# A chunked linear-attention and MLP kernel: the third pair's loads reordered and gated behind a second-stage product, three buffers of stacked v, and a new hand-written order

## The chip, the cores and the metric

The kernel runs on one core of one Trainium2 chip. The metric is device time in microseconds (us). TensorE (PE in the profile) multiplies matrices, VectorE (DVE), ScalarE (ACT) and GpSimd (POOL) do the elementwise work, and SyncE (SP) issues most of the DMA transfers. All engines run beside each other, each one in its own program order, and wait for one another through semaphores.

## The reference

Two stages follow each other. First a recurrent attention with decay, over 4 batches, 8 heads, 768 tokens and a head size of 48; then a two-layer MLP with the gate h * cos(h) on all 3072 tokens.

```
for t in range(S):
    state = alpha[:, :, t, :, None] * state + einsum('bhd,bhe->bhde', k[:, :, t], v[:, :, t])
    y[:, :, t] = einsum('bhd,bhde->bhe', q[:, :, t], state)
x = y.transpose(0, 2, 1, 3).reshape(3072, 384)
h = x @ w_in            # 384 x 2048
out = (h * cos(h)) @ w_out   # 2048 x 384
```

## The kernel before

The 3072 tokens are cut into 12 pairs J of two chunks, 256 tokens each, three pairs to a batch. On the partitions lie 128 pairs of neighbouring tokens e = 0, 1; the chunk c is a half of the partitions, 64 rows each. The steps of one pair, by the names that the plan uses, are these.

- `load` (L110) brings alpha (`a`), k, q and v, 384 KB each, in one DMA each from SP's queue. `w1` (L126) and `w2` (L132) bring the weights in four quarters each, issued by GpSimd, which also changes them to bf16.
- `ln` (L146) takes the logarithm of alpha, `cums0` and `cums` (L168, L182) sum it over the tokens with triangular matrices on TensorE, and `icp`, `exps` (L209, L219) exponentiate the sums. For pairs from 3 on, `eb` bundles these and the next pair's `ln`, `mula` (L154) multiplies neighbouring alphas ahead of it, and `sub` (L199) takes one alpha off again.
- `sk` (L233) and `sq` (L237) scale k and q into the tiles kh and qh, on DVE or POOL, once for each e. `castv` (L240) casts v.
- `trans` (L288) transposes kh and qh with 32 small matmuls into PSUM, and `evT` (L294) copies each chunk out. `scores` (L303) multiplies them, `mask` (L309) applies the causal mask on DVE.
- `outer` (L321) makes the sums of k times v, `add` (L335, L337) adds the state before, and `state` (L343) decays it on POOL.
- v is stacked in another order for the last product: by four SP DMAs (`vst`, L246) or, for the first three pairs, by TensorE and a copy (`vpe` L256, `vev` L260). Two buffers `vs` hold it; a buffer is free again when the `yT` that reads it is done.
- `yT` (L370) makes the attention's output, transposed, and `evy` (L379) copies it to bf16.
- `m1` (L390) is a first-stage product: for each pair four units u, of 12 matmuls 128x128 by 128x256 each. `sin` (L396) takes the cosine on ACT, `gate` (L401) multiplies on DVE. `m2` (L419) is the second stage: for each pair two tiles c, each in four parts of four matmuls. `evo` (L431) copies the result out and `out` (L437) stores it.
- `idle` (L445) are products on zeros that keep TensorE busy at the start.

In PSUM, three buffers of two banks with the tag `h` serve the transposes, the scores, the sums, yT and the first-stage products in turn: a step that wants one waits until the reader of the buffer has finished, and a first-stage product's buffer becomes free with its gate.

The order is written out by hand. The table `PLAN` gives each step of each pair a number; all steps are sorted by it and issued in that order, with `:A` or `:D` naming another engine than the usual one. The numbers are no times: they only set the program order on every engine and on SP's and POOL's DMA queues. `GATES` makes one load wait for a step on TensorE, and since SP works in order, all loads behind it wait as well. The tile pools decide on further waits: the raw k, q and v have three buffers each and alpha four.

On ACT, logarithm and exponential belong to one table and the cosine to another; going over from one to the other costs a table load (L141 and L396).

Of the kernel before, what the change touches and what calls it, by code (L numbers as in the profile page):

```python
# [16 lines left out]
def kernel(  # L17
# [26 lines left out]
    NL, NQ, NV, NS = 4, 3, 3, 2  # L44
# [35 lines left out]
    for lst, nm, n in ((lna_t, "lna", NL), (kh_t, "kh", NQ), (qh_t, "qh", NQ), (vp_t, "vp", NV)):  # L80
        for r in range(n):
            t = consts.tile([C, 2, H, 64], BF, tag=f"{nm}{r}", name=f"{nm}{r}")
            nc.vector.memset(t[:, :, :, D:64], 0.0)
            lst.append(t)
# [14 lines left out]
    GATES, AFTER = {("a", 2): ("yT", 1)}, {}  # L99
# [7 lines left out]
    def load(nm, J):  # L107
        b, g = J // NJB, J % NJB
        t = sb.tile([C, H, 2, D], FP, tag=nm, name=nm, bufs=BUF["a" if nm == "a" else "in"])
        dma = nc.sync.dma_start(  # L110
# [120 lines left out]
    def scale_k(J, e, eng):  # L231
        icp_ = icp_sb.pop((J, e)).rearrange("p (h d) -> p h d", h=H)
        eng.tensor_tensor(out=kh_t[J % NQ][:, e, :, 0:D], in0=kqv["k", J][:, :, e], in1=icp_, op=ALU.mult)  # L233

    def scale_q(J, e, eng):
        cp = cp_sb[J, e][:, 0:HD].rearrange("p (h d) -> p h d", h=H)
        eng.tensor_tensor(out=qh_t[J % NQ][:, e, :, 0:D], in0=kqv["q", J][:, :, e], in1=cp, op=ALU.mult)  # L237
# [43 lines left out]
    def trans(J):  # L281
        T_ps[J] = ps.tile([C, 2, 2 * NP, 2, HC], BF, tag="h", name="T_ps", bufs=3)
        for i, x in ((1, kh_t[J % NQ]), (0, qh_t[J % NQ])):
            for p in range(NP):
                for e in range(2):
                    for c in range(2):
                        r = slice(HC * c, HC * c + HC)
                        last = nc.tensor.transpose(T_ps[J][:, c, i * NP + p, e, :],  # L288
                                            x[r, e, 2 * p : 2 * p + 2, :].rearrange("s h d -> s (h d)"), ident_bf[r, r])
# [23 lines left out]
    def outer(J):  # L313
# [3 lines left out]
        for p in range(NP):  # L317
            for e in range(2):
                for c in range(n):
# [3 lines left out]
                        kh[r, e, 2 * p : 2 * p + 2, :].rearrange("s h d -> s (h d)"),  # L323
# [61 lines left out]
    def mlp1(J, u):  # L385
        h_ps[J, u] = ps.tile([C, FW, T2], FP, tag="h", name="h_ps", bufs=3)
        for f in range(FW):
            ft = u * FW + f
            for kk in range(KT):
                nc.tensor.matmul(h_ps[J, u][:, f, :], w1[:, kk, ft * C : (ft + 1) * C], xT[J][:, kk, :],  # L390
                                 start=(kk == 0), stop=(kk == KT - 1))

# [15 lines left out]
    def mlp2(J, c, part):  # L408
# [8 lines left out]
        for o, cols in zip(o_ps[J, c], HALVES if last_tile else [slice(0, DM)]):  # L417
            for ft in fts:
                nc.tensor.matmul(o[:, 0 : cols.stop - cols.start], gsb[J][:, ft, c * C : (c + 1) * C], w2[:, ft, cols],  # L419
                                 start=(done == 1 and ft == fts[0]), stop=(done == MP and ft == fts[-1]))  # L420

# [19 lines left out]
    def idle(n):  # L441
# [5 lines left out]
    copies = {"DVE": nc.vector.tensor_copy, "ACT": nc.scalar.copy}  # L447
    mults = {"DVE": nc.vector, "POOL": nc.gpsimd}
    steps = {
        "load": lambda J, nm: load(nm, J), "w1": load_w1, "w2": load_w2,  # L450
# [4 lines left out]
        "evT": lambda J, c, eng="DVE": evict_T(J, c, copies[eng]), "scores": scores, "mask": mask, "outer": outer,  # L455
# [71 lines left out]
    }  # L527
    IDLE = [(45, 10), (155, 2), (345, 9), (375, 1), (435, 4), (485, 3)]
# [45 lines left out]
```

## Time and profile before

| | us |
|---|---|
| median of three runs (185.56 to 185.94) | 185.88 |
| the profiled execution | 185.78 |
| its span, first to last instruction | 184.0 |
| busy TensorE / VectorE / ScalarE / GpSimd | 173.0 / 134.5 / 124.9 / 83.5 |
| idle products on zeros, within TensorE's busy time | 9.0 |
| first first-stage product starts | 17.3 |
| last TensorE matmul ends | 180.8 |

All times in the text are counted from the span's first instruction. The profile has a page and views of the trace: busy times by stage (windows), the instructions of one engine in order of time (timeline), groups of instructions by line, tile views, and the DMA issues with the time from issue to landing. In the rows of a timeline stand start, duration, engine, line, operation, output<-inputs, their shapes, the count (x12), and in brackets how long the engine sat idle before and what ended that. In the rows of groups stand the busy time, the mean of one in ns, and the idle time before them.

### The profile page before, as it was taken

What the parts mean: (1) busy time and instruction counts of PE and PEld (TensorE: products, weight loads), DVE (VectorE), ACT (ScalarE), POOL (GpSimd) and SP (SyncE); (2) the same over time, 40 slices, a digit from 0 to 9 for tenths busy, and PEclk for the clock granted to TensorE, in tenths of its full rate; (3) what the DMA queues carried; (4) which work ended last, traced back from release to release, by engine and by line L of the source; (5) the groups of instructions that cost most, each with busy time, mean ns of one, the idle gap of its engine ahead of it and who ended that gap; (6) DMA issues with size and microseconds to landing.
All of it is one profiled execution on the core that took longest, in us unless ns stands there. A gap on an engine that the chain in (4) does not pass through costs nothing.

```text
span 184.0 us, 5742 instructions
## 1 busy us (share of the span) xinstructions
PE 173.0 (94%) x2457; PEld 125.5 (68%) x2458; DVE 134.5 (73%) x182; ACT 124.9 (68%) x157; POOL 83.5 (45%) x116
## 2 busy tenths in 40 slices
PE   7989579979999999999999999999899999999993
PEld 2445458646687776876787777876687677776672
DVE  7069777669999899799969898879587674734520
ACT  3745457789879999895978989869774517435201
POOL 5388550079883484939686093903901110000000
PEclk9999999999999999999999999999999999999999
DMA  6999999999999979963996579003420121010312
GB/s 146 261 248 224 216 202 206 262 256 257 261 213 262 304 170 278 260 164 85 278 289 154 140 215 245 18 6 88 143 71 4 41 88 51 0 43 4 127 44 86
DMA packets 60137, 29.47 MB, mean 160 GB/s; under 512 B 51024, under 2 KB 60112, under 8 KB 60112
## 3 DMA queue, kind: packets, MB, share of 16 engines
q1 hardware_dynamic: 56256, 25.86, 57.9%
q0 software_dynamic: 3712, 3.15, 10.6%
q8 instruction: 19, 0.31, 0.8%
q10 hardware_dynamic: 144, 0.10, 0.2%
q14 instruction: 6, 0.05, 0.1%
HBM read 25.17 MB, written 4.72 MB: 162 GB/s over the span
## 4 chain that ended last, share of the span: by engine, by line
PE 68%; DMA 11%; issue 7%; SPq 6%; POOL 5%; ACT 1%; DVE 1%; POOLq 0%; DVEq 0%
PE h_ps L390 28%; PE o_ps L419 26%; DMA v<-in_v_dram 6%; SPq L110 4%; PE y_ps L370 4%; DMA k<-in_k_dram 4%; PE A_ps L303 2%; PE T_ps L288 2%; PE U_ps L321 2%; SPq L246 2%; PE o_last L419 1%; DMA vs<-vp 1%; POOL un L343 1%; POOL a L154 1%; PE cums L168 1%
## 5 line engine op out<-in xcount | busy, mean ns | idle before, releaser
L401 DVE TENSOR_TENSOR gsb<-h_ps,c_sb 128x1024 bf16<-128x1024 f32 x48 | 58.4, 1222 | 20.0 <-ACT c_sb L396 18.8
L396 ACT ACTIVATE c_sb<-h_ps,halfpi 128x1024 bf16<-128x1024 f32 x48 | 53.4, 1114 | 28.5 <-PE h_ps L390 28.4
L390 PE MATMUL h_ps<-xT,w 128*128 128x256 bf16 x576 | 67.5, 273 | 0.7 <-DMA w<-in_moe_w_in_dram 0.5
L419 PE MATMUL o_ps<-w,gsb 128*128 128x384 bf16 x368 | 66.7, 326 | 0.0
L390 PEld LDWEIGHTS <-w 128*128 128x128 bf16 x576 | 55.4, 98 | 9.7 <-DMA w<-in_moe_w_in_dram 0.8
L419 PEld LDWEIGHTS <-gsb 128*128 128x128 bf16 x400 | 37.0, 98 | 20.8
L343 POOL TENSOR_TENSOR un<-us,c 128x384 bf16<-128x384 f32 x20 | 16.7, 836 | 33.1 <-DVE us L335 26.0
L309 DVE TENSOR_TENSOR A_sb<-A_ps,msk 128x1024 bf16<-128x1024 f32 x24 | 29.1, 1220 | 3.6 <-PE A_ps L303 3.4
L233 POOL TENSOR_TENSOR kh<-k,icp 128x384 bf16<-128x384 f32 x19 | 19.5, 1032 | 10.2 <-ACT lna L146 5.3
L237 POOL TENSOR_TENSOR qh<-q,cp 128x384 bf16<-128x384 f32 x19 | 18.8, 999 | 6.1 <-ACT cp L219 4.2
L154 POOL TENSOR_TENSOR a<-a 128x384 f32<-128x384 f32 x9 | 9.0, 997 | 11.8 <-DMA a<-in_alpha_dram 11.8
L240 POOL CAST vp<-v 128x768 bf16<-128x768 f32 x12 | 10.1, 853 | 6.4 <-DMA v<-in_v_dram 6.0
L146 ACT ACTIVATE lna<-a 128x768 bf16<-128x768 f32 x12 | 10.1, 842 | 4.1 <-DMA a<-in_alpha_dram 2.4
L141 ACT ACT_TABLE_LOAD x9 | 11.5, 1283 | 0.9 <-PEq L558 0.7
L294 DVE COPY qkT<-T_ps 128x1024 bf16<-128x1024 bf16 x17 | 11.4, 682 | 0.8 <-PE T_ps L288 0.8
L396 ACT ACT_TABLE_LOAD x9 | 11.5, 1283 | 0.2
L431 ACT COPY o_sb<-o_ps 128x384 f32<-128x384 f32 x10 | 4.8, 478 | 9.6 <-PE o_ps L419 9.6
L431 DVE COPY o_sb<-o_ps 128x384 f32<-128x384 f32 x13 | 7.2, 554 | 4.3 <-PE o_ps L419 4.2
L445 PE MATMUL idle_ps<-zeros 128*128 128x512 bf16 x28 | 9.0, 469 | 1.2 <-DVE halfpi L77 1.2
L379 DVE CAST xT<-y_ps 128x384 bf16<-128x384 f32 x14 | 7.7, 584 | 3.1 <-PE y_ps L370 2.9
L335 DVE TENSOR_TENSOR us<-U_ps,un 128x384 f32<-128x384 f32 x16 | 8.8, 551 | 1.3 <-PE U_ps L321 1.2
L303 PE MATMUL A_ps<-qkT 48*128 48x128 bf16 x192 | 8.7, 217 | 0.6 <-DVE qkT L294 0.5
(68 smaller groups left out, 149.2 us busy)
## 6 DMA issues: line engine op xcount, KB each, us to landing
a<-in_alpha_dram SPq DMA_DIRECT2D x12, 384.0 KB, 6.0
v<-in_v_dram SPq DMA_DIRECT2D x12, 384.0 KB, 6.1
k<-in_k_dram SPq DMA_DIRECT2D x12, 384.0 KB, 6.0
q<-in_q_dram SPq DMA_DIRECT2D x12, 384.0 KB, 6.2
out_dram<-o_sb SPq DMA_DIRECT2D x23, 192.0 KB, 2.3
vs<-vp SPq DMA_DIRECT2D x36, 64.0 KB, 2.8
w<-in_moe_w_in_dram POOLq DMA_DIRECT2D x4, 384.0 KB, 8.7
w<-in_moe_w_out_dram POOLq DMA_DIRECT2D x4, 384.0 KB, 10.7
```

What stands on the lines that cost most here:

```text
L141: nc.scalar.preload_act_table_set("natural_log_exp_and_others")
L233: eng.tensor_tensor(out=kh_t[J % NQ][:, e, :, 0:D], in0=kqv["k", J][:, :, e], in1=icp_, op=ALU.mult)
L237: eng.tensor_tensor(out=qh_t[J % NQ][:, e, :, 0:D], in0=kqv["q", J][:, :, e], in1=cp, op=ALU.mult)
L294: ins = copy(out=qkT_sb[J][:, c], in_=T_ps[J][:, c].rearrange("r n e s -> r n (e s)"))
L303: last = nc.tensor.matmul(A_ps[J, c][:, a, p, :], qkT[r, c, NP + p, :], qkT[r, c, p, :], start=True, stop=True)
L309: nc.vector.tensor_tensor(out=A_sb[J][:, c].rearrange("s a p t -> s (a p) t"), in0=A_ps.pop((J, c)).rearrange("s a p t -> s (a p) t"), in1 ...
L343: nc.gpsimd.tensor_tensor(out=u, in0=U_sum.pop(n), in1=c2_sb[J][:, :, c].unsqueeze(3).to_broadcast([C, NP, 2, D]), op=ALU.mult)
L390: nc.tensor.matmul(h_ps[J, u][:, f, :], w1[:, kk, ft * C : (ft + 1) * C], xT[J][:, kk, :], start=(kk == 0), stop=(kk == KT - 1))
L396: nc.scalar.activation(out=c_sb[J, u], in_=h_ps[J, u], func=AF.Sin, bias=halfpi, scale=1.0)
L401: nc.vector.tensor_tensor(out=gsb[J][:, u * FW : (u + 1) * FW], in0=h_ps.pop((J, u)), in1=c_sb.pop((J, u)), op=ALU.mult)
L419: nc.tensor.matmul(o[:, 0 : cols.stop - cols.start], gsb[J][:, ft, c * C : (c + 1) * C], w2[:, ft, cols], start=(done == 1 and ft == fts[0 ...
L431: copy(out=t, in_=o_ps.pop((J, c))[0][:, 0:DM])
```

## The change

- SP's first loads come in another order: v1, a1, a0, v0, k0, q0, q1, k1, a2, q2 (the number is the pair) in place of a0, a1, v0, k0, q0, k1, q1, v1, q2.
- The gate is another one. Before, a2 waited for the yT of pair 1. Now a2 and q2 wait for no step; a3, k3, q3, v3 and a4 wait for the part 3 of the second-stage product of pair 0, tile 0 (`m2 0 0 3`). On SP a3 stands before k2 and v2, which so come behind it too.
- GpSimd issues the weights in one run behind the casts of v1 and v0, with two short steps between: w1 quarters 1, 0, 3, 2, then w2 quarters 3, 2, 1, 0.
- The stacked v has three buffers in place of two (NS), with one more memset on POOL.
- kh and qh are laid out by head pair, then e, in place of e, then head.
- A step `tr` that transposes by DMA is defined, but the plan does not hold it.
- The whole plan is new: the position of every step, and the engine of some. Among others, on DVE the scaling of pair 1's k (`sk 1 1`, `sk 1 0`) comes before `mask 0 1` of pair 0; on ACT `ln 2` comes before the first cosine. 44 idle products stand in the plan in place of 29.

```
-    NL, NQ, NV, NS = 4, 3, 3, 2
+    NL, NQ, NV, NS = 4, 3, 3, 3
...
-            t = consts.tile([C, 2, H, 64], BF, tag=f"{nm}{r}", name=f"{nm}{r}")
+            t = consts.tile([C, 2, H, 64] if nm in ("lna", "vp") else [C, H, 2, 64], BF, tag=f"{nm}{r}", name=f"{nm}{r}")
             nc.vector.memset(t[:, :, :, D:64], 0.0)
-            lst.append(t)
+            lst.append(t.rearrange("s (p e) a d -> s p e a d", p=NP) if nm in ("kh", "qh") else t)
...
-    GATES, AFTER = {("a", 2): ("yT", 1)}, {}
+    GATES, AFTER = {('a', 3): ('m2', 0, 0, 3), ('k', 3): ('m2', 0, 0, 3), ('q', 3): ('m2', 0, 0, 3), ('v', 3): ('m2', 0, 0, 3), ('a', 4): ('m2', 0, 0, 3)}, {}
...
+        pass_gate(("m2", J, c, part), last)
...
-        "load a": "10 20 960 1030 1170 1450 1460 2230 2570 2290 3490 2960",
-        "load k": "70 190 1040 1270 1530 2020 1990 3050 3500 4180 3440 4290",
-        "load q": "100 230 300 1290 1620 1950 2580 2850 3980 4010 3970 4770",
-        "load v": "40 290 1130 1220 1730 1930 1940 3090 3680 2990 4970 4850",
-        "w1": "330 200 470 460 - - - - - - - -",
-        "w2": "260 580 820 690 - - - - - - - -",
+        "load a": "40 20 670 1160 1370 1780 2170 2320 2730 2910 3970 3890",
+        "load k": "200 450 1210 1470 1810 2250 2750 2760 3580 3620 4400 4680",
+        "load q": "300 410 1010 1510 1880 2220 2440 3320 3020 3720 4270 3490",
+        "load v": "90 10 1290 1710 1950 2700 2310 3650 4150 4730 5300 5110",
+        "w1": "120 110 230 220 - - - - - - - -",
+        "w2": "490 460 400 320 - - - - - - - -",
...
-        "ln": "30 110 1060 1100 - - - - - - - -",
+        "ln": "50 30 740 1180 - - - - - - - -",
...
-        "sk 1": "250 280 1350:D 1560:D 2100 2260 2890:D 3340 3890 4510 4890 5480",
+        "sk 1": "270:D 510:D 1250 1490:D 2090 2260 2900 3180:D 3960 4080 4780 4910",
...
-        "castv": "90 610 1210 1260 2120 2750 2720 3760 3730 4980 5000 5360",
+        "castv": "100 80 1300 1720 1970 3090 2860 3670 4160 4750 5310 5710",
-        "vst": "- - - 1820 2320 3120 3110 4040 4450 5160 5010 5380",
+        "vst": "- - - 2060 2280 3350 3290 4310 4770 5050 5320 5730",
...
-        "mask 1": "430 720 1600 1870 2420 3390 3540 4110 4470 5070 5100 5880",
+        "mask 1": "560 700 1450 1760 2300 3480 3430 4190 4410 5070 5470 5860",
...
-        "yT": "490 780 1750 2150 2790 3570 3620 4330 4870 5170 5670 5970",
+        "yT": "600 760 1630 2070 2650 3550 3520 4320 4950 5130 5630 5900",
...
-        "m1 0": "740 940 2000 2520 2980 3670 3900 4620 5150 5610 5900 6040",
-        "m1 1": "560 890 1960 2400 2950 3860 3750 4630 5250 5390 5850 6090",
+        "m1 0": "810 1140 1890 2430 2960 3760 3790 4590 5080 5570 5830 6390",
+        "m1 1": "710 930 1830 2670 2840 3730 3660 4740 5290 5440 6010 6080",
...
-        "sin 1": "570 900 1970 2410 2970 3870 3790 4690 5280 5400 5860 6100",
+        "sin 1": "790 940 1840 2680 2920 3740 3700 4850 5330 5450 6030 6090",
...
-        "m2 0 3": "1010 1510 2350 2770 3410 4300 4830 5440 5720 6120 6320 6550",
+        "m2 0 3": "950 1560 2370 3000 3450 4200 4940 5400 5800 6160 6340 6540",
...
-    IDLE = [(45, 10), (155, 2), (345, 9), (375, 1), (435, 4), (485, 3)]
+    IDLE = [(55, 17), (275, 7), (385, 5), (435, 6), (525, 2), (575, 5), (595, 2)]
```

More of the change, by code (lines that the diff above doesn't have):

```diff
@@ L105, in pass_gate, with load @@
                 AFTER[key] = last
-    def load(nm, J):
+    def load(nm, J, queue):
         b, g = J // NJB, J % NJB
         t = sb.tile([C, H, 2, D], FP, tag=nm, name=nm, bufs=BUF["a" if nm == "a" else "in"])
-        dma = nc.sync.dma_start(
+        dma = queue.dma_start(
             out=t.rearrange("p h e d -> p h (e d)"),
@@ L232, in scale_k @@
         icp_ = icp_sb.pop((J, e)).rearrange("p (h d) -> p h d", h=H)
-        eng.tensor_tensor(out=kh_t[J % NQ][:, e, :, 0:D], in0=kqv["k", J][:, :, e], in1=icp_, op=ALU.mult)
+        eng.tensor_tensor(out=kh_t[J % NQ][:, :, e, :, 0:D], in0=kqv["k", J][:, :, e].rearrange("p (n a) d -> p n a d", a=2),
+                          in1=icp_.rearrange("p (n a) d -> p n a d", a=2), op=ALU.mult)
     def scale_q(J, e, eng):
         cp = cp_sb[J, e][:, 0:HD].rearrange("p (h d) -> p h d", h=H)
-        eng.tensor_tensor(out=qh_t[J % NQ][:, e, :, 0:D], in0=kqv["q", J][:, :, e], in1=cp, op=ALU.mult)
+        eng.tensor_tensor(out=qh_t[J % NQ][:, :, e, :, 0:D], in0=kqv["q", J][:, :, e].rearrange("p (n a) d -> p n a d", a=2),
+                          in1=cp.rearrange("p (n a) d -> p n a d", a=2), op=ALU.mult)
     def cast_v(J):
@@ L288, in trans, with trans_dma @@
                         last = nc.tensor.transpose(T_ps[J][:, c, i * NP + p, e, :],
-                                            x[r, e, 2 * p : 2 * p + 2, :].rearrange("s h d -> s (h d)"), ident_bf[r, r])
+                                            x[r, p, e].rearrange("s a d -> s (a d)"), ident_bf[r, r])
+    def trans_dma(J, x, c):
+        if J not in qkT_sb:
+            qkT_sb[J] = sb.tile([C, 2, 2 * NP, C], BF, tag="qkT", name="qkT", bufs=BUF["qkT"])
+        r = slice(HC * c, HC * c + HC)
+        i, src_t = {"k": (1, kh_t), "q": (0, qh_t)}[x]
+        nc.sync.dma_start_transpose(
+            out=qkT_sb[J][:, c, i * NP : (i + 1) * NP, :].rearrange("r n (e s) -> r (n e) s", e=2),
+            in_=src_t[J % NQ][r].rearrange("s p e a d -> s (p e a d)"))
     def evict_T(J, c, copy):
@@ L322, in outer @@
                         U_ps[J][:, c, 2 * p * D : 2 * (p + 1) * D].rearrange("r (a d) -> r a d", a=2),
-                        kh[r, e, 2 * p : 2 * p + 2, :].rearrange("s h d -> s (h d)"),
+                        kh[r, p, e].rearrange("s a d -> s (a d)"),
                         vp[r, e, 2 * p : 2 * p + 2, 0:D], start=(e == 0), stop=(e == 1))
@@ L389, in mlp1 @@
             for kk in range(KT):
-                nc.tensor.matmul(h_ps[J, u][:, f, :], w1[:, kk, ft * C : (ft + 1) * C], xT[J][:, kk, :],
+                last = nc.tensor.matmul(h_ps[J, u][:, f, :], w1[:, kk, ft * C : (ft + 1) * C], xT[J][:, kk, :],
                                  start=(kk == 0), stop=(kk == KT - 1))
+        pass_gate(("m1", J, u), last)
     def cosine(J, u):
@@ L418, in mlp2 @@
             for ft in fts:
-                nc.tensor.matmul(o[:, 0 : cols.stop - cols.start], gsb[J][:, ft, c * C : (c + 1) * C], w2[:, ft, cols],
+                last = nc.tensor.matmul(o[:, 0 : cols.stop - cols.start], gsb[J][:, ft, c * C : (c + 1) * C], w2[:, ft, cols],
                                  start=(done == 1 and ft == fts[0]), stop=(done == MP and ft == fts[-1]))
+        pass_gate(("m2", J, c, part), last)
     def evict_o(J, c, copy):
@@ L447 @@
     copies = {"DVE": nc.vector.tensor_copy, "ACT": nc.scalar.copy}
+    queues = {"SP": nc.sync, "POOL": nc.gpsimd}
     mults = {"DVE": nc.vector, "POOL": nc.gpsimd}
     steps = {
-        "load": lambda J, nm: load(nm, J), "w1": load_w1, "w2": load_w2,
+        "load": lambda J, nm, eng="SP": load(nm, J, queues[eng]), "w1": load_w1, "w2": load_w2,
         "mula": mul_a, "ln": ln, "cums0": cums0, "cums": cums, "sub": sub, "icp": icp, "exps": exps, "eb": session,
@@ L454 @@
         "vev": lambda J, eng="DVE": evict_vs(J, copies[eng]), "decay": decay, "trans": trans,
-        "evT": lambda J, c, eng="DVE": evict_T(J, c, copies[eng]), "scores": scores, "mask": mask, "outer": outer,
+        "evT": lambda J, c, eng="DVE": evict_T(J, c, copies[eng]), "tr": trans_dma, "scores": scores, "mask": mask, "outer": outer,
         "add": add_state, "state": decay_state, "yT": yT, "evy": lambda J, c, eng="ACT": evict_y(J, c, copies[eng]),
```

96 rows, old and new, of the table PLAN are left out of this document.

## The prediction

> **What bounds the kernel now.** First the page, then the busy times by stage, then TensorE's own timeline.
>
> ```profile
> span 184.0 us, 5742 instructions
> PE 173.0 (94%) x2457; PEld 125.5 (68%) x2458; DVE 134.5 (73%) x182; ACT 124.9 (68%) x157; POOL 83.5 (45%) x116
> ```
> ```profile
> 0.00:27.15 27.15, 21.41 (x324) 12.44 (x326) 18.06 (x46) 13.83 (x20) 17.06 (x36) 1.00 1.14 216
> 27.15:34.36 7.21, 7.21 (x64) 6.28 (x65) 5.51 (x5) 5.75 (x6) 0.00 (x0) 1.00 1.24 230
> 34.36:60.00 25.64, 24.34 (x401) 17.02 (x399) 21.16 (x29) 21.73 (x30) 17.92 (x20) 1.00 1.10 249
> 120.00:130.00 10.00, 9.22 (x181) 6.11 (x179) 8.46 (x10) 8.51 (x12) 2.94 (x5) 1.00 0.25 55
> 170.00:184.00 14.00, 10.84 (x87) 7.76 (x84) 3.92 (x5) 2.15 (x4) 0.00 (x0) 0.99 0.23 84
> ```
> ```profile
> 0.00:34.36 34.36, 11.16 (x96) 7.93 (x7) 7.80 (x7) 1.00 1.16 219
> ```
> ```profile
> 24.61 0.63 PE L370 MATMUL y_ps<-A_sb,vs 128*32 128x128 bf16 x32
> 25.18 1.48 PE L390 MATMUL h_ps<-xT,w 128*128 128x256 bf16 x12
> 27.15 5.42 PE L390 MATMUL h_ps<-xT,w 128*128 128x256 bf16 x48 [0.49 <-DMA w<-in_moe_w_in_dram]
> ```
> A window's row gives its length, then PE, PEld, DVE, ACT and POOL busy, the clock, the DMA share and GB/s. TensorE (PE) sets the time. From 27.15 on it hardly stops: nothing is lost to 34.36, 1.30 us from there to 60, 0.78 in the window from 120, and 3.16 in the tail. Its work is the same matrix products in both kernels, so the change can move the end in three ways: by when PE gets going, by waits in the middle, and by that 0.78. The front is the large item: of the 21.41 busy us ahead of 27.15 much is idle products on zeros. The second fence is the window to 34.36 for the tile h_ps alone (PE, DVE, ACT): 96 matmuls, eight first-stage products of 12. Four run from 27.15 (1.31 each: 5.42 less the modelled overlap of 0.16), one more by 34.36, so three stand ahead of 27.15 and two ahead of 25.18.
>
> What sets the front is when loads land.
>
> ```profile
> 7.21 1.45 SPq L110 DMA_DIRECT2D q<-in_q_dram  x1
> 8.70 1.44 SPq L110 DMA_DIRECT2D v<-in_v_dram  x1
> 10.18 1.40 SPq L110 DMA_DIRECT2D q<-in_q_dram  x1
> ```
> ```profile
> q<-in_q_dram SPq DMA_DIRECT2D x1, 384.0 KB, 6.2
> v<-in_v_dram SPq DMA_DIRECT2D x1, 384.0 KB, 10.9
> q<-in_q_dram SPq DMA_DIRECT2D x1, 384.0 KB, 16.3
> ```
> ```profile
> 4.43 0.84 ACT L146 ACTIVATE lna<-a 128x768 bf16<-128x768 f32 x1 [2.41 <-DMA a<-in_alpha_dram]
> 7.49 0.82 POOL L240 CAST vp<-v 128x768 bf16<-128x768 f32 x1 [4.29 <-DMA v<-in_v_dram]
> 8.55 0.93 POOL L126 DMA_DIRECT2D w<-in_moe_w_in_dram  x1
> 9.03 0.56 DVE L233 TENSOR_TENSOR kh<-k,icp 128x384 bf16<-128x384 f32 x1 [4.49 <-DMA k<-in_k_dram]
> 12.09 1.95 POOL L233 TENSOR_TENSOR kh<-k,icp 128x384 bf16<-128x384 f32 x2 [0.76 <-DMA k<-in_k_dram]
> ```
> The second fence is the DMA view (KB, us from issue to landing) in the windows around the 7th, 8th and 9th issue. Loads 1, 3, 4 and 6 land at 4.43, 7.49, 9.03 and 12.09: 1.5 us apart. The 7th lands at 7.21 + 6.2 = 13.4. The 8th takes 10.9 us, to 19.6, and the 9th 16.3, to 26.5: the weights, issued by GpSimd from 8.55 on, have begun to move. The DMA queues in the windows 11 to 12, 12 to 13 and 13 to 14 (packets, MB, share) show it:
>
> ```profile
> q1 hardware_dynamic: 694, 0.26, 127.5%
> ```
> ```profile
> q1 hardware_dynamic: 407, 0.15, 74.5%
> q0 software_dynamic: 91, 0.09, 55.5%
> ```
> ```profile
> q0 software_dynamic: 201, 0.21, 123.1%
> q1 hardware_dynamic: 4, 0.00, 0.9%
> ```
> The inputs alone move 0.26 MB per us (a load is 0.39 MB); once the weights come they move nothing from 13 to 14.
>
> **The change, part by part.** *Load order.* SP now issues v1, a1, a0, v0, k0, q0, q1, k1, a2, q2, with v1 the second pair's v. The positions land as before: v0, now 4th, at 9.0, k0 at 10.5, q0 at 12.1, q1 at 13.4. k1 is 8th, in the place where v1 took until 19.6; a2 is 9th.
>
> *Weights.* They are issued behind the casts of v1 and v0 on POOL: 9.03 + 0.82 is 9.85, which is 1.3 us after 8.55. Before, their first bytes came in the window from 12 (about 12.2 by the 0.09 MB); now about 13.5. k1 then has its first 0.12 MB through at full rate. The remaining 0.27 MB, and the hole behind it, I scale from the 8th load before (6.2 us from the 7th's landing to its own): two thirds of that is 4.2, so 17.6, and I take **17.9**, between 15 (no sharing: 13.4 + 1.5) and 19.6 (as before), nearer the row that shows sharing. a2 comes 26.5 - 19.6 = 6.9 later: **24.8**, between 3 later (equal shares) and 26.5.
>
> *New order, behind k1.* On DVE, sk 1 1 waits for k1, and queued behind it are sk 1 0, add 0 0 and mask 0 1 of the *first* pair, which its yT needs. Before, that mask ran ahead of all second-pair work. Durations:
>
> ```profile
> L401 DVE TENSOR_TENSOR gsb<-h_ps,c_sb 128x1024 bf16<-128x1024 f32 x48 | 58.4, 1222 | 20.0 <-ACT c_sb L396 18.8
> L396 ACT ACTIVATE c_sb<-h_ps,halfpi 128x1024 bf16<-128x1024 f32 x48 | 53.4, 1114 | 28.5 <-PE h_ps L390 28.4
> L309 DVE TENSOR_TENSOR A_sb<-A_ps,msk 128x1024 bf16<-128x1024 f32 x24 | 29.1, 1220 | 3.6 <-PE A_ps L303 3.4
> L141 ACT ACT_TABLE_LOAD x9 | 11.5, 1283 | 0.9 <-PEq L558 0.7
> L294 ACT COPY qkT<-T_ps 128x1024 bf16<-128x1024 bf16 x7 | 7.0, 1010 | 1.9 <-PE T_ps L288 1.8
> L335 DVE TENSOR_TENSOR us<-U_ps,un 128x384 f32<-128x384 f32 x16 | 8.8, 551 | 1.3 <-PE U_ps L321 1.2
> ```
> ```profile
> 8.44 2.10 PE L445 MATMUL idle_ps<-zeros 128*128 128x512 bf16 x9
> 16.45 0.41 PE L288 MATMUL T_ps<-ident_bf,kh 64*128 64x64 bf16 x16
> 24.28 0.52 PE L370 MATMUL y_ps<-qkT,un 128*32 128x128 bf16 x24 [0.53 <-DVE A_sb L309]
> ```
> With K the landing of k1: two scalings (0.56 each, pipelined) K+1.05; the 32 transposes K+1.65; the first eviction on ACT K+2.75; scores K+3.2; two idle matmuls (0.23 each) K+3.65; yT of pair 0 to K+4.45, whose mask was ready at K+2.8 (add 0.55, mask 1.22). DVE goes add, mask 1 0 (to K+4.6), xT, add, mask 1 1 (to K+6.95); PE meanwhile does outer 1, scores and one first-stage product (to K+6.65). yT of pair 1 (0.9) ends at K+7.95 = **25.85**. Before it ended at 24.61 + 0.63 = 25.2 with two products done; now one is.
>
> *ln 2 moves ahead.* On ACT it now stands in front of the first cosine and waits for a2. Behind it: ln 0.84 (the 4.43 row), table load 1.28, cosine 1.11, then gate 1.22 on DVE: 24.8 + 4.5 = 29.3. That gate frees the PSUM buffer for the fourth product, which PE would reach at 25.85 + 2 x 1.31 = 28.45: a wait of **0.85**. Then the fourth to sixth product (3.9) and one second-stage part (0.65, half of a product, as 4 x 384 columns are to 12 x 256) end at 33.9, and the gate on SP opens. At 34.36 the old kernel had done that and two products more; it had the same work done 2.62 earlier, at 31.75. Loss: 33.9 - 31.75 = **+2.15**.
>
> *The gate.* a3 waits for that part, and all later loads stand behind it on SP, k2 and v2 among them. Before, the gate opened at the first row; the second gives the landing times of the loads of alpha:
>
> ```profile
> 25.30 0.99 SPq L110 DMA_DIRECT2D a<-in_alpha_dram  x2
> ```
> ```profile
> DMA to landing us min/median/max: 3.7/6.0/10.6
> ```
> By 33.9 the weights are nearly in (eight of 0.39 MB at 0.2 MB per us is 15.7, plus 2.7 loads of 1.5, from 13.5 on: 33.3), so a3 lands by the short end, 3.7, at 37.6, k2 at 39.1, v2 at 40.6. PE has 7.6 us of older products first (two first-stage, six second-stage, the sums), to 41.55, and sk 2 1 (1.0 on POOL) ends at 40.1: hidden, with 1.4 to spare. Three waits remain by the same reckoning: ln 3 behind two table loads and two cosines on ACT (0.5), ln 4 behind the next session (0.5), yT 2 behind four scalings on DVE (0.45). 1.45 against 1.30 before: **+0.15**.
>
> *Third stacked v.* Before, pair 10's stacking waits for yT 8, and pair 9's stands behind it on SP:
>
> ```profile
> 122.99 5.70 SPq L246 DMA_DIRECT2D vs<-vp  x8
> 130.04 0.75 PE L370 MATMUL y_ps<-A_sb,vs 128*32 128x128 bf16 x32 [0.80 <-DMA vs<-vp]
> ```
> With three buffers it needs yT 7 only: **-0.8**. The added memset (0.3) lies before the first cast, where POOL waits 4.29.
>
> *At nothing:* the layout of qh and kh (same element and instruction counts; each transpose and outer product still reads 128 adjacent columns; if the longer pattern cost POOL 0.1 us each, 33 of them would still lie in an engine 45% busy); the DMA transpose, which the plan never calls; 15 more idle matmuls (3.5 us), all beside waits but the two in the sum; five evictions of T moved to ACT (0.33 longer each), off the path after the front; the tail, whose last products and store are the same.
>
> Sum: 2.15 + 0.15 - 0.8 = **+1.5** on the profiled execution's 185.78 (span 184.0 and 1.78 around it; 0.10 under the median of 185.88): **187.3**.
>
> **Rivals.** *Equal turns, faster.* If the weights and inputs take turns evenly, the rest of k1 (0.27 MB) moves at 0.13 per us and lands by 16.5, a2 by about 20. Then DVE is the floor: mask 0 0 ends at 16.7 (q0 12.1, scaling to 13.5, transposes 14.0, eviction 15.0, scores 15.5, mask 1.22). yT 1 ends at 24.65, no wait on ACT: loss 2.15 - 1.2 - 0.85 = 0.1, in all -0.55, **185.2**. The sum turns at K = 17.25 with a2 in time. For it: from 12 to 13 both queues moved; against it: the hole from 13 to 14 and the 9th load's 16.3 us. The Trainium skill, "DMA: Bandwidth & Descriptors", section "Queues, rings and completion order", says that each DMA engine goes round the queues with work packet by packet, which would bring about this rival; the 8th and 9th load bear it out poorly. 24%.
> *The gate bites.* If weights still move when it opens, a3 takes 10.6 as before and k2 lands at 46, PE waits 4 to 5 us at trans 2: **191.5**. Against it: the DMA reckoning above. 8%.
> *Absorbed.* The middle waits are set by loads and ACT, so a PE that comes 2 us later may find them gone: -1.3, **186.0**, no difference. Against it: a3 and ln 3 come later too. 10%.
>
> **How the numbers follow.** The forecast has 58%. Its own range: K from 16.9 to 19.6, a2 to 26.5: 186.2 to 189.3. With the equal turns at the low end and some new wait of the rearranged order at the high end: **185.0 to 189.6**; the gate's 191.5 and the rest are left out. A difference under 0.2% (0.37 us) cannot be told from none here. Faster 0.18 (most of the equal turns), same 0.15 (their rest, and most of the absorbed case), slower 0.67.
>
> **What would show it.** Load 8 (k1) landing near 18 and a2 near 25; DVE idle before sk 1 1; ACT idle before ln 2 and PE before the fourth first-stage product; yT 1 ending near 26; SP's gate near 34; sk 2 without a long wait for k2; no PE wait for vs. Wrong, if k1 lands before 17, or if PE waits over 2 us between 35 and 50.

## The result and the profile after

The changed kernel takes 185.14 us (median of five runs, 184.87 to 185.21) beside 185.88 for the kernel before on the same chip (five runs, 185.56 to 185.99): a ratio of 0.9963, with a 95% interval of 0.9949 to 0.9978. That is 0.4% faster, where 187.3, slower by 0.8%, was forecast. Of the page, two lines:

```profile
span 183.4 us, 5755 instructions
PE 175.2 (96%) x2470; PEld 126.1 (69%) x2473; DVE 132.6 (72%) x182; ACT 126.0 (69%) x160; POOL 78.8 (43%) x112
```

The span is 0.6 us shorter. TensorE still sets it. The same windows as in the prediction (length, PE, PEld, DVE, ACT, POOL busy, clock, DMA share, GB/s):

```profile
0.00:27.15 27.15, 23.78 (x337) 13.30 (x341) 16.63 (x46) 13.65 (x20) 15.36 (x35) 1.00 1.13 215
27.15:34.36 7.21, 5.80 (x55) 4.74 (x55) 6.46 (x6) 5.99 (x7) 0.00 (x0) 1.00 1.14 177
34.36:60.00 25.64, 25.38 (x407) 18.21 (x406) 21.47 (x30) 23.85 (x33) 14.85 (x17) 1.00 1.10 251
120.00:130.00 10.00, 10.00 (x206) 6.73 (x204) 8.12 (x11) 8.10 (x11) 7.24 (x9) 1.00 0.37 86
```

The front does lose: TensorE stops for 1.41 us in the second window, where the old kernel lost nothing. But the third loses 0.26 instead of 1.30, and the fourth nothing instead of 0.78. The instructions behind this, from the timelines of SP, POOL, DVE, ACT and PE (start, duration, engine, line, operation, in brackets the idle time before and what ended it):

```profile
8.78 1.44 SPq L110 DMA_DIRECT2D k<-in_k_dram  x1
10.26 1.39 SPq L110 DMA_DIRECT2D a<-in_alpha_dram  x1
...
9.84 3.25 POOL L126 DMA_DIRECT2D w<-in_moe_w_in_dram  x4
...
16.63 1.02 DVE L233 TENSOR_TENSOR kh<-k,icp 128x384 bf16<-128x384 f32 x2
...
23.98 0.85 ACT L146 ACTIVATE lna<-a 128x768 bf16<-128x768 f32 x1 [2.20 <-DMA a<-in_alpha_dram]
...
23.76 0.63 PE L381 MATMUL y_ps<-A_sb,vs 128*32 128x128 bf16 x32
24.32 2.79 PE L401 MATMUL h_ps<-xT,w 128*128 128x256 bf16 x24
28.56 4.09 PE L401 MATMUL h_ps<-xT,w 128*128 128x256 bf16 x36 [1.44 <-DVE gsb L413]
32.49 0.81 PE L431 MATMUL o_ps<-w,gsb 128*128 128x384 bf16 x4
...
42.40 0.32 PE L168 MATMUL cums<-lna,tri 128*128 128x384 bf16 x1 [0.26 <-ACT lna L146]
```

The DMA view of the windows around the two issues (KB, us to landing) gives the landings:

```profile
k<-in_k_dram SPq DMA_DIRECT2D x1, 384.0 KB, 6.2
a<-in_alpha_dram SPq DMA_DIRECT2D x1, 384.0 KB, 13.7
```

k1 landed at 8.78 + 6.2 = 15.0, not at 17.9; VectorE scales it without a stop at 16.63, right behind the mask of the first pair, and yT 1 ends at 23.76 + 0.63 = 24.39, not at 25.85. a2 landed at 10.26 + 13.7 = 23.96 (24.8 forecast), ScalarE waits 2.20 for it, and through ln 2, the table load, the first cosine and its gate TensorE waits 1.44 ahead of the fourth first-stage product. The gating part of the second stage ends at 33.14 (32.49 + 0.81 less the modelled overlap of 0.16); the old kernel had that work done at 31.75: +1.39, not +2.15.

### The profile page after: what moved, and what is told of

The parts are those of the page before. It is cut to its first block, busy times and chain, and to the rows that moved or that the text cites. A ratio compares the mean times of both kernels' runs of the same rounds, so it can differ in the third digit from the quotient of the medians.

```text
span 183.4 us, 5755 instructions
## 1 busy us (share of the span) xinstructions
PE 175.2 (96%) x2470; PEld 126.1 (69%) x2473; DVE 132.6 (72%) x182; ACT 126.0 (69%) x160; POOL 78.8 (43%) x112
## 4 chain that ended last, share of the span: by engine, by line
PE 77%; DMA 7%; ACT 6%; SPq 5%; issue 1%; DVE 1%
PE h_ps L401 31%; PE o_ps L431 31%; DMA a<-in_alpha_dram 7%; SPq L110 5%; PE y_ps L381 5%; PE A_ps L314 3%; PE T_ps L290 3%; ACT c_sb L408 2%; PE U_ps L332 2%; PE o_last L431 1%; ACT L141 1%; ACT L408 1%; PE cums L168 1%; DVE gsb L413 1%; ACT lna L146 0%
## 5 line engine op out<-in xcount | busy, mean ns | idle before, releaser
L401 PEld LDWEIGHTS <-w 128*128 128x128 bf16 x576 | 55.2, 98 | 10.7 <-issue 1.9
L238 POOL TENSOR_TENSOR qh<-q,cp 128x384 bf16<-128x384 f32 x17 | 16.9, 1000 | 20.1 <-ACT cp L219 20.1
L233 POOL TENSOR_TENSOR kh<-k,icp 128x384 bf16<-128x384 f32 x16 | 16.2, 1020 | 7.5 <-DMA k<-in_k_dram 3.7
L305 ACT COPY qkT<-T_ps 128x1024 bf16<-128x1024 bf16 x12 | 11.8, 1013 | 5.7 <-PE T_ps L290 5.6
L444 ACT COPY o_sb<-o_ps 128x384 f32<-128x384 f32 x13 | 6.2, 480 | 11.1 <-PE o_ps L431 11.1
L458 PE MATMUL idle_ps<-zeros 128*128 128x512 bf16 x41 | 12.2, 442 | 1.7 <-DVE halfpi L77 1.2
L390 DVE CAST xT<-y_ps 128x384 bf16<-128x384 f32 x16 | 8.9, 586 | 3.8 <-PE y_ps L381 3.8
L233 DVE TENSOR_TENSOR kh<-k,icp 128x384 bf16<-128x384 f32 x8 | 4.2, 552 | 7.4 <-DMA k<-in_k_dram 7.4
L458 PEld LDWEIGHTS <-zeros 128*128 128x128 bf16 x44 | 4.2, 109 | 7.0 <-issue 3.0
## 6 DMA issues: line engine op xcount, KB each, us to landing
w<-in_moe_w_in_dram POOLq DMA_DIRECT2D x4, 384.0 KB, 10.7
```

Source lines behind the costliest of these rows:

```text
L233: eng.tensor_tensor(out=kh_t[J % NQ][:, :, e, :, 0:D], in0=kqv["k", J][:, :, e].rearrange("p (n a) d -> p n a d", a=2), in1=icp_.rearrange ...
L238: eng.tensor_tensor(out=qh_t[J % NQ][:, :, e, :, 0:D], in0=kqv["q", J][:, :, e].rearrange("p (n a) d -> p n a d", a=2), in1=cp.rearrange(" ...
L305: ins = copy(out=qkT_sb[J][:, c], in_=T_ps[J][:, c].rearrange("r n e s -> r n (e s)"))
L401: last = nc.tensor.matmul(h_ps[J, u][:, f, :], w1[:, kk, ft * C : (ft + 1) * C], xT[J][:, kk, :], start=(kk == 0), stop=(kk == KT - 1))
L458: nc.tensor.matmul(idle_ps[0], zeros[:, 0:C], zeros, start=True, stop=True)
```

## The experiments

The theory: the front costs 1.39, set by a2 alone; the middle gives back 1.04, because the old order's stop at cums 3 is gone; the stop for the stacked v gives about 1. The rivals: the order alone does what the third buffer is credited with; the moved gate alone empties the middle; pair 2's loads set the old middle whatever the order; the two DMA queues share by bytes. Each kernel computes everything; times are medians, the ratio is to the kernel before on the same chip. The runs stood on several chips, so that two of them are compared by their ratios or their traces. The lines of the plan are cut to the positions that differ.

**Three buffers alone, and the change without them.** The kernel before with `NS = 3`:

```
-    NL, NQ, NV, NS = 4, 3, 3, 2
+    NL, NQ, NV, NS = 4, 3, 3, 3
```

> The kernel before with three buffers of stacked v and nothing else. Theory A (the wait of 0.8 us at 130 came from the two buffers: the stacking of pair 10 waited for yT 8 and held that of pair 9 behind it on SP): the wait goes, 185.1 against 185.9. Rival B (the new order removed it, the stacking is late for another reason): the wait stays, 185.9.

184.31 us, 0.9922 (0.9905 to 0.9939): 0.8 less than expected, and more than the whole change gains. In its timeline of TensorE the stop is gone; the same product started at 130.04 in the kernel before:

```profile
128.79 0.62 PE L370 MATMUL y_ps<-A_sb,vs 128*32 128x128 bf16 x32
```

Of these 1.25 us, 0.27 were ahead already at pair 8's yT (122.06, 122.33 before); by pair 10's (144.09, 145.48 before) the buffer's share is 1.39 - 0.27 = 1.12: in the kernel before, pair 9's product starts 0.98 late (1.25 - 0.27) and takes 0.75 in place of 0.62. The opposite edit to the changed kernel, `NS = 2`:

> The changed kernel with two buffers of stacked v. Theory A (the third buffer is worth 0.8 us in the new order too): 185.9. Rival B (in the new order each stacking stands close before its own yT and after the yT two pairs earlier, so two buffers do as well): within 0.2 us of the changed kernel, 185.1.

185.05 us, 0.9971 (0.9957 to 0.9984): no different from 185.14. Its window from 120 to 130 has no stop either:

```profile
120.00:130.00 10.00, 10.00 (x217) 6.81 (x218) 8.11 (x12) 7.83 (x11) 7.24 (x9) 1.00 0.36 85
```

In the new order the third buffer is worth nothing: order and buffer remove the same stop, and either one is enough.

**The gate alone**, in the old order: a2 free, a3 behind yT 1.

```
-    GATES, AFTER = {("a", 2): ("yT", 1)}, {}
+    GATES, AFTER = {("a", 3): ("yT", 1)}, {}
```

> The kernel before with its gate moved from a2 to a3, still behind yT 1: a2 goes out early, as the tenth load. Theory A (before, PE waited 1.0 us for ln 3 because a3 stood behind a2 in a queue that the weights slowed, and landed at 36.4): a3 lands about 1.5 us earlier, ln 3 is no longer late, about 1.0 us faster, 184.9. Rival B (that wait hangs on the place of cums 3 in PE's order, a table load and mula ahead of it on ACT and POOL): the wait stays within 0.3 us, 185.6 to 185.9. A loss is possible if q2, ninth, and a2, tenth, slow the weights that PE waits for at 27.

185.85 us, 1.0022 (1.0002 to 1.0041). Its windows:

```profile
27.15:34.36 7.21, 6.37 (x57) 5.52 (x58) 4.75 (x4) 5.09 (x5) 0.00 (x0) 1.00 1.26 204
34.36:60.00 25.64, 25.24 (x408) 17.64 (x406) 21.69 (x29) 22.43 (x31) 17.70 (x20) 1.00 1.10 246
```

0.84 is lost in the front: a2 now moves beside the weights, and the last first-stage quarter, issued at about 16.4, lands 11.5 us later in place of 10.7. 0.90 is won in the middle (0.40 lost, not 1.30). Theory A's reason does not hold: a3 lands no earlier, as pair 3's `mula` on POOL shows, which waits for it (36.39 in the kernel before):

```profile
36.61 0.99 POOL L154 TENSOR_TENSOR a<-a 128x384 f32<-128x384 f32 x1 [11.32 <-DMA a<-in_alpha_dram]
```

cums 3 starts at 38.53 (38.31 before), though TensorE comes 0.84 later: a TensorE that comes later finds the old middle's stop gone.

**The weights later, in the new order.** In all three, all quarters of w1 stand behind the first pair's decay on GpSimd, which moves the first issue from 9.84 to 12.5. The first leaves three quarters of w2 right behind them:

```
-        "w1": "120 110 230 220
-        "w2": "490 460 400 320
+        "w1": "342 341 344 343
+        "w2": "490 460 400 345
```

> The changed kernel with the first five weights issued behind decay 0 on POOL, at about 12.2 in place of 9.84. Theory A (weights begin to move 4.1 us after their issue; until then inputs move at 0.26 MB per us, from then on at about 0.06): a2 is through before they begin and lands near 16.5 in place of 24.0, the cosine goes 1.7 us earlier, PE's wait of 1.4 us before the fourth first-stage product goes: 183.8. The weights land 1 to 2.4 us later and still in time. Rival B (the wait hangs on the table load behind ln 2 on ACT, or the weights come too late then): 185 or more.

184.71 us, 0.9953 (0.9938 to 0.9968), where 183.8 was expected. a2 took 6.2 us and the 1.44 were gone, but seven issues in a row hold up GpSimd's scaling of q:

```profile
19.10 0.41 PE L290 MATMUL T_ps<-ident_bf,qh 64*128 64x64 bf16 x16 [1.02 <-POOL qh L238]
```

The second has that scaling first:

```
-        "w2": "490 460 400 320
+        "w2": "490 483 482 481
```

> The changed kernel with weights behind decay 0, as in the run before, and POOL's scaling sq 1 0 ahead of the four second-stage weights. In the run before PE waited 1.0 us at the transposes of pair 1 for that scaling, which stood behind seven weights. Theory A (the front is then free of both waits): 183.7. Rival B (the second-stage weights come too late for m2 0 0 3, or ACT's chain holds the front anyway): 184.5 or more.

184.62 us, 0.9942 (0.992 to 0.9965), where 183.7 was expected. Now the first pair's state stood behind four issues and VectorE waited 1.37 for it. The third spreads them in pairs behind the states:

```
-        "w2": "490 460 400 320
+        "w2": "736 735 633 632
```

> The changed kernel with the first-stage weights behind decay 0 and sq 1 0 next, as before, and the second-stage weights in two pairs behind the states of pair 0. Before, PE gained 0.7 us of the 1.4 at the end of the front, as the first state stood behind four weights on POOL and yT 1 came 0.9 later. Theory A: yT 1 ends at 24.4 as in the changed kernel, no wait for a2, the gate opens at 31.7, 183.6. Rival B (the middle gives it back: ln 3 and the inputs of pair 2 come no earlier): the wait at cums 3 grows, 184.4 or more.

183.61 us, 0.9886 (0.9863 to 0.9909), as expected, and the best of all. Its timeline of TensorE and its windows:

```profile
24.34 6.73 PE L401 MATMUL h_ps<-xT,w 128*128 128x256 bf16 x60
30.90 0.81 PE L431 MATMUL o_ps<-w,gsb 128*128 128x384 bf16 x4
```
```profile
27.15:34.36 7.21, 7.21 (x68) 5.88 (x67) 5.98 (x5) 6.57 (x8) 0.00 (x0) 1.00 1.22 205
34.36:60.00 25.64, 25.28 (x410) 17.68 (x407) 22.34 (x31) 23.86 (x35) 14.92 (x18) 1.00 1.07 248
```

Five first-stage products run without a stop and the gating part ends at 30.90 + 0.81 - 0.16 = 31.55, 1.59 earlier than in the changed kernel, and the middle still loses only 0.36. So the whole +1.39 hung on a2's landing, and in this order the front counts to the end: the spans of the profiled executions are 183.4 and 181.8, and by the ratios the difference is 1.4.

**The weights earlier, in the new order**, as a test of how two queues share:

```
-        "w1": "120 110 230 220
+        "w1": "87 86 89 88
```

> The changed kernel with the four first-stage weights issued between the casts of v1 and v0, from about 5.4 on in place of 9.84. Theory A (from about 4 us after, inputs move packet for packet with the weights, some 6.5 us for each load): k0, q0, q1 and k1 are slow, k1 lands near 28 in place of 15.0, and the kernel takes 194 to 198. Rival B (equal shares in bytes, 3 us for each load): k1 near 20, 188 to 190.

198.88 us, 1.0707 in one round of two executions, a little above theory A's 194 to 198. k1 landed at 30.3, where packets in strict turn had it near 28. Its DMA queues from 12 to 14 (packets, MB, share), and VectorE:

```profile
q0 software_dynamic: 298, 0.30, 87.5%
q1 hardware_dynamic: 296, 0.11, 32.1%
```
```profile
30.30 1.03 DVE L233 TENSOR_TENSOR kh<-k,icp 128x384 bf16<-128x384 f32 x2 [3.17 <-DMA k<-in_k_dram]
```

**Shorter fronts in the old order.** With three buffers, a quarter of w1 later, then w1 ahead of w2:

```
-        "w1": "330 200 470 460
+        "w1": "330 255 470 460
```

> The kernel before with three buffers of stacked v and the first weight one POOL step later, behind sk 0 1, at about 10.5 in place of 8.55. Theory A (a weight begins to move about 4 us after its issue, and only from then on the inputs are slow): v1, the eighth load, lands at about 15.2 in place of 19.4; q2, ninth, still takes long. The time gains little of it, as the cast of v1 stands behind weight issues on POOL until 18, and the last first-stage weight comes up to 2 us later than 27: 184.0 to 185.5. Rival B (the eighth load is slow by its place in SP's queue, whatever the weights do): v1 lands at 19 or later.

184.41 us, 0.9933 (0.9909 to 0.9956): v1, the 8th load, took 6.2 us instead of 10.9, but TensorE waited 2.2 for weights. With that, and a clock of 0.76 from 22 to 26, the gating part starts 1.36 later than in e1 (33.69, 32.33), and still the time is only 0.1 longer, as the middle loses 0.18 where e1's loses 1.16:

```profile
34.36:60.00 25.64, 25.46 (x413) 18.08 (x412) 22.30 (x30) 23.21 (x31) 17.68 (x20) 1.00 1.08 242
```

This is e3's finding once more: the old middle gives back what the front loses.

```
-        "w1": "330 200 470 460
-        "w2": "260 580 820 690
+        "w1": "260 255 470 460
+        "w2": "575 580 820 690
```

> As the run with the first weight later, and the second-stage quarter 0 behind all four first-stage quarters on POOL. Theory A (PE's last wait of the front, 0.6 us at 27, is for the fifth weight; as fourth it comes about 2 us earlier): PE runs without a stop from about 25, 183.0. Rival B (the front of the old order is set by the cast of v1 and its chain): 184.2, as with three buffers alone.

184.30 us, 0.993 (0.9905 to 0.9956), as e1. Sixty first-stage matmuls run from 25.08 without a stop (e1: 48 from 27.07), and the gating part starts at 31.64, 0.69 ahead of e1's, and yet cums 3 starts nearly where it did in e1 (38.21) and in the kernel before (38.31):

```profile
38.10 0.32 PE L168 MATMUL cums<-lna,tri 128*128 128x384 bf16 x1 [1.40 <-ACT lna L146]
```

There cums 3 waits for ln 3, and that for a3, which moves among the weights. The kernel before, POOL and ACT:

```profile
36.39 0.99 POOL L154 TENSOR_TENSOR a<-a 128x384 f32<-128x384 f32 x1 [10.79 <-DMA a<-in_alpha_dram]
```
```profile
37.41 0.84 ACT L146 ACTIVATE lna<-a 128x768 bf16<-128x768 f32 x1 [1.52 <-POOL a L154]
```

**What holds the old middle.** With three buffers, pair 3's cums moved later, to just ahead of pair 2's transposes (40.64 and 40.98 in the first), and its sub with it; then its ln too; then ln with e7's weights:

```
-        "cums": "140 210 1080 1120        "sub": "- - - 1200
+        "cums": "140 210 1080 1325        "sub": "- - - 1330     (cums alone)
+        "cums": "140 210 1080 1335        "sub": "- - - 1337     (with ln 3 from 1100 to 1332)
```

> The kernel before with three buffers of stacked v, cums 3 moved on PE behind the second tile of pair 0, sub 3 with it on DVE. Theory A (the middle is held by pair 2's scalings, whose exponentials stand behind ln 3 on ACT, which waits for a3): PE waits at trans 2 in place of cums 3, 184.0 to 184.3. Rival B (only the place of cums 3 on PE costs the 1.0 us): the wait goes, 183.3.

> As the run with cums 3 later, and ln 3 moved on ACT behind the four exponentials of pair 2, as in the changed kernel. Theory A (the 1.0 us of the old middle came from ln 3 ahead of pair 2's exponentials): no wait over 0.3 us from 34 to 60, 183.3. Rival B (pair 2's k and v land too late anyway): 184.0 or more.

> The same with the first-stage weights ahead of the second-stage ones, which made the front 1.5 us shorter before and won nothing, as cums 3 started at 38.1 whatever the front did. Theory A (with ln 3 out of the way the shorter front counts): 182.0. Rival B (the loads of pair 2, behind the gate at yT 1 and the weights, hold the middle at the same time of the clock): 183.3, as with ln 3 alone.

184.64 (0.9936, 0.9911 to 0.996), 184.58 (0.9938, 0.9918 to 0.9957) and 184.33 (0.9924, 0.9904 to 0.9945). None gains on e1's 0.9922; in each profile the stop of 1.0 had moved to pair 2's transposes. In all three sub 3 stands ahead of pair 2's scaling on VectorE and waits for the later cums 3, so that the first meets theory A's stop for another reason than ln 3. The timeline of the second:

```profile
40.60 0.56 DVE L199 TENSOR_TENSOR cp<-cums,lna 128x384 f32<-128x384 f32 x1 [1.46 <-PE cums L182]
41.08 0.55 DVE L233 TENSOR_TENSOR kh<-k,icp 128x384 bf16<-128x384 f32 x1
...
41.69 0.38 PE L288 MATMUL T_ps<-ident_bf,kh 64*128 64x64 bf16 x14 [1.05 <-DVE kh L233]
```

The clock in all three profiles was low from 22 to 26 (0.61, 0.57, 0.58), and TensorE came to the middle late. So these runs said nothing on what they were made for; the following ones have sub 3 behind that scaling (1355 in place of 1337), without and with e7's weights:

> The kernel before with three buffers of stacked v (184.3 alone), and pair 3's ln, cums and sub moved behind pair 2's transposes, with sub 3 now also behind sk 2 1 on VectorE. Theory A (in the old middle nothing but the place of pair 3's alpha steps holds TensorE: cums 3 behind ln 3, and, once that is moved, kh of pair 2 behind sub 3): TensorE's stop of 1.0 us ahead of trans 2 goes too, the window 34.36 to 60 loses about 0.3 instead of 1.3, and the time is 183.3. Theory B (pair 2's k and q land too late in the old order, so that trans 2 waits for them whatever stands ahead): a stop of about 1 us stays at trans 2 and the time stays at 184.3 to 184.6. If the clock at 22 to 26 us is below full in the profiled execution, about 1.2 us is lost there and says nothing on either theory.

> The same, and with the weights in the order that made the old front 1.5 to 2 us shorter with no gain at the end (184.3). Theory A (the shorter front was given back at cums 3 alone): with that stop gone the front counts, and the time is 182 to 182.5. Theory B (the loads of pair 2 set the old middle): what the front gains comes back as a longer stop at trans 2 (1.5 to 2.5 us there), and the time stays at 184.3.

184.13 (0.9921, 0.9897 to 0.9944) and 184.09 (0.9915, 0.9895 to 0.9934): both ratios lie within e1's interval. The first bears out A's mechanism, not its time: the stop of 1.0 is gone, and the window loses 0.63 in place of e1's 1.16:

```profile
34.36:60.00 25.64, 25.01 (x406) 17.86 (x405) 21.91 (x29) 22.55 (x31) 17.74 (x20) 1.00 1.07 244
```

But its profiled execution had a clock of 0.61 from 22 to 26, its gating part starts 0.34 later than e1's (32.67, 32.33), and a late TensorE alone shrinks the loss, as e6 shows. The second ran at full clock there. Its gating part starts at 31.48, 0.85 ahead of e1's, and the big stop is gone as well, but the window still loses 1.17, and neither theory holds. Its window and its stops on TensorE:

```profile
34.36:60.00 25.64, 24.47 (x399) 17.16 (x397) 21.21 (x29) 21.74 (x31) 17.85 (x20) 1.00 1.14 250
```
```profile
39.86 0.38 PE L288 MATMUL T_ps<-ident_bf,kh 64*128 64x64 bf16 x14 [0.21 <-DVE kh L233]
44.75 0.32 PE L168 MATMUL cums<-lna,tri 128*128 128x384 bf16 x1 [0.17 <-ACT lna L146]
...
47.16 0.38 PE L288 MATMUL T_ps<-ident_bf,qh 64*128 64x64 bf16 x14 [0.21 <-POOL qh L237]
...
50.69 0.62 PE L303 MATMUL A_ps<-qkT 48*128 48x128 bf16 x16 [0.43 <-ACT qkT L294]
```

Four small stops take part of the lead away: pair 2's scaling, ln 4, pair 3's scaling and its eviction all stand just behind. Of the 0.85, 0.38 is left at pair 2's first-stage products (51.25, 51.63 in e1) and 0.4 in the spans (182.2, 182.6), too little to be told in the times. So none of the single waits that were moved holds the old middle by itself; in the new order a shorter front reaches the end whole (e9).

## Why the prediction was wrong

The forecast was +1.5, and the two profiled executions differ by -0.57. Of these 2.07 the middle makes 1.19, the front 0.76, and the stacked v, with all that comes behind 60 us, 0.11. The middle is the step that turned the sign.

**The bound** was right: TensorE, the front, the middle and the one stop past 120 are where the time moved.

**K, the landing of k1** (step *Weights*) failed: 15.0, not 17.9, and a K before 17 was one of the prediction's signs of being wrong. The weights' first packets came as I had them, from 13.5 to 13.7, and in numbers from about 13.9, 4.1 us after the issue at 9.84. The term that failed is the 0.12 MB that I let k1 have through by then. In the kernel before, the inputs' queue had moved 2.73 MB by 12.5, when the weights came in numbers: seven loads, and nothing of the 8th. In the changed kernel the weights came 1.4 us later, and by 14 the queue had moved 3.12 MB, eight loads: hardly anything of k1 was left to share. From 13 to 14 the inputs still moved at nearly full rate (DMA queues of the changed kernel, the windows from 13, 14 and 18 on, the last 2 us long):

```profile
q1 hardware_dynamic: 649, 0.25, 121.0%
q0 software_dynamic: 14, 0.01, 8.5%
```
```profile
q0 software_dynamic: 183, 0.19, 112.0%
q1 hardware_dynamic: 83, 0.03, 14.5%
```
```profile
q0 software_dynamic: 304, 0.30, 87.3%
q1 hardware_dynamic: 304, 0.12, 33.1%
```

By itself this error changed nothing at the end: yT 1 came 1.46 earlier than forecast, and TensorE only waited longer at the fourth product, 1.44 in place of 0.85, for the gate that hangs on a2.

**The front's +2.15** was +1.39. The mechanism (ln 2 waits for a2, then table load, cosine, gate, fourth product) was right; the mis-sized term is a2's landing, 23.96 for 24.8: the wait ends 0.74 earlier (28.56 for 29.3), and the sum is 0.76 smaller. That a2 came so near is partly luck: I had it 6.9 behind k1, and it came 9.0 behind a k1 that was 2.9 early. In e9, where a2 comes early, the front loses nothing (31.55 beside 31.75).

**The gate** was right: a3 issued at 33.33 (33.9), landed in 3.8 us (3.7), k2 in 5.5, at about 39.3 (39.1), with no stop for them on TensorE. The margin of 1.4 was not there, though: POOL's scaling of k2 ends at 40.72, and the transposes start at 40.61.

**The middle's +0.15** failed most: -1.04. I reckoned three new waits of about 0.5 in place of the old 1.30; of the three only cums 3's came, at 0.26, and cums 4 (46.09) and yT 2 (47.67) start without a stop. The new order keeps its middle nearly free, and not because TensorE comes late: e9's front is as short as the old one, and its middle loses only 0.36. Which of its moves do so was not separated and stays open. The rival called *absorbed*, at 10%, named a mechanism that exists, as e3 and e6 show in the old order, where a later TensorE finds the stop gone; e9 shows that the changed kernel does not need it.

**Third stacked v, -0.8**: the stop went, but alone it is worth 1.1 (e1), as pair 9's product started 0.98 late and took longer; and in the new order the gain is the order's (e2).

Together: by the front and the middle TensorE is 1.39 - 1.04 = 0.35 behind at 60 us, and its last sixteen matmuls start 0.56 ahead (178.79, 179.35 before), so 0.91 is gained between, most of it the stop of 0.78 (the forecast had 0.8). The medians differ by 0.74, the profiled executions by 0.57.

*Equal turns* gave 185.2, nearly the time, for another reason: its early k1 came from the bytes that were through before the weights and not from even sharing, it had a2 at 20, which landed at 24, and its -0.55 rests on a front that loses 0.1 and a middle at +0.15. Turns are what the queues take once both are in full flow: 304 packets each from 18 to 20, 298 and 296 in e8. That agrees with the rule of the Trainium skill that the rival leant on ("DMA: Bandwidth & Descriptors", "Queues, rings and completion order": round the queues packet by packet); whether the profile's packets are the page's is not shown. In the weights' first 2 us it was not so: 183 to 83 from 14 to 15, and 201 to 4 from 13 to 14 in the kernel before; why stays open. And a packet of the weights carries 2.5 times the bytes (0.30 MB to 0.12 in as many packets), so equal turns are not equal rates: the inputs get 0.06 MB per us, at which one load takes 6.5 us. I had taken turns for bytes.

*At nothing* held as far as it shows: no stop on TensorE was due to layout, idle products or moved evictions.

## What to carry to other kernels

Follow a delay through to the step where the next wait ends, and ask at each old wait whether it is still there once the engine comes later; where the next stage waits for something else, a loss in front of it is partly given back, and so is a gain. Try the small parts of a large change by themselves: one more buffer in the old order gave 1.3 us (the whole change 0.7), and the new order with the weights spread gave 2.1. When two DMA queues share, compare packet sizes before rates.

## What the runs showed of the hardware

- The weights move in numbers 3.6 to 4.1 us after GpSimd issues the first of them (8.55 to 12.5 before, 9.84 to 13.9 after, 12.49 to 16.1 in e9), so inputs whose bytes are through by then still land at full rate (a2 in e4 and e9: 6.2 us).
- Several weight issues in a row occupy GpSimd for 0.8 us each (3.25 for four), and its elementwise work stands behind them (1.02 and 1.37 us of waits in e4 and e5).
- TensorE's granted clock fell without a long stop in some executions (0.57 to 0.61 from 22 to 26 in the profiles of e10 to e13). In e12's, the windows from 18 and 22:

```profile
18.00:22.00 4.00, 2.75 (x48) 2.13 (x48) 3.08 (x5) 2.26 (x3) 2.62 (x4) 1.00 1.23 222
22.00:26.00 4.00, 3.63 (x57) 2.65 (x56) 2.48 (x4) 0.89 (x1) 2.42 (x3) 0.58 1.28 203
```

Twelve matmuls took 2.60 us there instead of 1.47, behind stops of 1.03 and 0.37. e14 had stops of 1.03, 0.37 and 0.22 at the same place and kept 1.00. What decides there stays open. Behind a long stop, in e8, TensorE's rows are slow as well; the same five idle products take 1.25 us in e4:

```profile
20.49 0.61 PE L290 MATMUL T_ps<-ident_bf,qh 64*128 64x64 bf16 x16 [7.36 <-DVE qh L238]
21.03 2.31 PE L458 MATMUL idle_ps<-zeros 128*128 128x512 bf16 x5
```

The Trainium skill, "TensorE: Matmul & The Clock Gate", part 1, has the clock halve after an idle window of some 3.4 us. The 2.31 us behind a stop of 7.36 are in accord with that (the clock from 20 to 30 was 0.79); e12's stops are far shorter.
